# A chunk of the second expert product moved from behind a branch to the end of the arm before it

## The chip, the cores and the metric

The kernel runs on one core of a Trainium2 chip. The metric is the device time of one execution in microseconds, the median of several runs. The engines are TensorE (PE in the profile, with PEld for the loading of its weights), VectorE (DVE), ScalarE (ACT), GpSimd (POOL) and SyncE (SP), which issues DMAs. Each works through its own queue in order and waits for the others by semaphores.

## The reference

```python
attn = sigmoid(q @ k.T / sqrt(64) - log(448))     # 4 batches, 12 heads, 448 x 64
x    = (attn @ v) as rows                         # 1792 tokens x 768
do   = x @ w_skip > 0                             # tokens that go to an expert
e    = argmax(x[do] @ w_gate)                     # one of 8 experts
gate = softmax value of that expert
x[do] += gate * (relu(x[do] @ w1[e]) @ w2[e])     # w1: 768 x 1024, w2: 1024 x 768
h    = x @ w_in                                   # 768 x 2048
out  = elu(h) @ w_out                             # 2048 x 768
```

All in float32. The kernel keeps this accuracy by splitting each operand into a high and a low part (`hi`, `lo`) and making three products: high by high, high by low, low by high.

## The kernel before

There are three stages: attention and the routing of tokens, the experts, and the last two products over all tokens. The change lies in the expert stage.

**Blocks and arms.** Tokens are sorted by expert into blocks of 256 slots, two halves of 128. How many blocks there are and how full each is is known on the chip alone, so `level(i, k)` (L1081) is a nest of branches. Each block takes one of three arms by the count `k`: the *single* arm (one half used, L1104), the *middle* arm (a full half and one of up to 64 tokens, `few`, L1096) or the *whole* arm (two full halves, `many`, L1100). In the profiled execution blocks 0 to 7 are whole, whole, middle, whole, middle, single, single, single.

**Where engines meet at a branch.** The code behind a branch must hold for either way through it. So each of the middle and whole arms has an `else` in which `rest()` (L1075) gives TensorE, ScalarE and VectorE one tiny instruction (L1077, L1078, L1079), and the code behind may wait for that instruction in place of what the arm would have done.

**Weights.** An expert's weights are eight chunks of 128 x 1536: 0 to 3 are w1, 4 to 7 are w2. SyncE loads them into 13 buffers. `split_w` (L722) makes the high part on ScalarE (L728, tile `whi`) and the low part on VectorE (L730, `wlo`). There are four pairs of split buffers, so chunk c takes the pair of chunk c - 4. `ahead` (L806) splits two chunks ahead of the products.

**A block, in the order of TensorE's queue.** `between` (L956) turns the block's rows of x: `columns` makes three groups of four 128 x 128 turnings, into `pt0`, `pt1` and `acc1`; ScalarE and VectorE split each into `x2` (L762, L763). Behind that stand chunks 5 and 6 of the *previous* block's first half (`back`, L860), the splits of chunks 0 and 1, and, behind the next branch in `lead_in`, chunk 7. Then the arm: the product with w1 (chunks 0 to 3), relu to `h2`, the product with w2 (chunks 4 to 7). In the single and middle arms the first product leaves rows, so h is turned into columns by `h_columns` (L770), half by half of F: for chunks 4 and 5 after chunk 2, for chunks 6 and 7 late in the arm. ScalarE and VectorE then write its high and low parts (L785, L786). A half of 128 tokens takes four groups of three products per w2 chunk (L737, L738, L739); a half of 64 takes four of two (L801, L802).

The first half's w2 product (`h` = 0 in the code) is spread so that TensorE has work across the branch: chunk 4 at the arm's end, 5 to 7 behind the next turning. The second half's stands wholly in the arm. `outcome` (L908) adds the gated sum to the rows on VectorE (L916); in the middle arm TensorE first doubles it up (L915), from a copy that ScalarE makes (L866). In block 0 `slot_order` (L1036) makes the order of the remaining rows: 12 small products into `acc1`, and seven VectorE instructions behind them (L1043 to L1054).

What sets the order of all this is the order of the code: TensorE, ScalarE and VectorE are scheduled by hand here.

Of the kernel before, what the change touches and what calls it, by code (L numbers as in the profile page):

```python
# [23 lines left out]
P = 128  # L24
# [10 lines left out]
KF1 = F1 // P  # L35
# [6 lines left out]
N2 = DM // 2  # L42
WCH = 1536
FA = 9
TB = 4
NOR = NTT // TB * TB
# [43 lines left out]
def build(nc, tc, a):  # L90
# [3 lines left out]
    with ExitStack() as top:  # L94
# [42 lines left out]
        def flip(dst, src):  # L137
            nc.tensor.transpose(dst, src, ident)  # L138
# [33 lines left out]
        with ExitStack() as st:  # L172
# [423 lines left out]
            for k_, p in enumerate(counted):  # L596
                nc.tensor.matmul(
                    ordered, ones_b, p, start=(k_ == 0), stop=(k_ == len(counted) - 1)
# [59 lines left out]
        with ExitStack() as st:  # L658
# [7 lines left out]
            def tiles(pool, names, shape, dt=F32):  # L666
                return [pool.tile([P, *shape], dt, name=n) for n in names]
# [16 lines left out]
            acc_t = tiles(psb, [f"acc{j}" for j in range(6)], [512])  # L684
            ends = (*pt_t, acc_t[1])
            py = [[acc_t[j][:, :N2] for j in js] for js in ((2, 3), (4, 1))]
# [81 lines left out]
                    split_columns(g, ends[g], x2)  # L768

            def h_columns(nh, sizes):  # L770
                for h, n in enumerate(sizes):
                    pt = pt_t[(nh + h) % 2].rearrange("p (c n) -> p c n", c=4)[:, :, :n]
                    for j in range(4):
                        w = slice(j * P, (j + 1) * P)
                        if n == P:
                            flip(pt[:, j, :], hs_t[nh][:, w])
                        else:
                            nc.tensor.matmul(
                                pt[:, j, :], hf_t[nh][:, w], fold[:, :n], start=True, stop=True
                            )  # L780
                    f, t = slice(4 * nh, 4 * nh + 4), slice(h * P, h * P + n)
                    h_hi, h_lo = h2[:, 0, f, t], h2[:, 1, f, t]
                    if n < P:
                        h_lo = h2[:, 0, f, h * P + n : (h + 1) * P]
                    nc.scalar.activation(h_hi, pt, AF.Relu)  # L785
                    nc.vector.scalar_tensor_tensor(  # L786
                        h_lo, pt, 0.0, h_hi, op0=ALU.max, op1=ALU.subtract
                    )

            def product(o, h, n, a2, i, c, width, k0, total):  # L790

                t = slice(h * P, (h + 1) * P)
                for j in range(WCH // width):
                    w = slice(j * width, (j + 1) * width)
                    hi, lo = (u[:, w] for u in weights(i, c))
                    a_hi, a_lo = a2[:, 0, k0 + j, t], a2[:, 1, k0 + j, t]
                    first, last = k0 + j == 0, k0 + j == total - 1
                    if n == P:
                        gemm(o, a_hi, a_lo, hi, lo, first, last)
                    else:  # L800
                        nc.tensor.matmul(o, a_hi, hi, start=first, stop=False, skip_group_check=True)  # L801
                        nc.tensor.matmul(  # L802
                            o[:n], a_hi[:, :n], lo, start=False, stop=last, skip_group_check=True
                        )
# [52 lines left out]
                        else:  # L857
                            nc.scalar.copy(hf_t[nh], acc_t[(3, 0)[nh]])

            def back(i, h, n, chunks):  # L860

                for c in chunks:
                    c4, nh = divmod(c - 4, 2)
                    product(py[nh][h], h, n, h2, i, c, N2, 4 * c4, KF1)
                    if n < P and c4:
                        nc.scalar.copy(yf_t[nh], py[nh][h])  # L866

            def expert(i, sizes, following=None):
                whole = sizes == (P, P)
                aside = places_in_order() if i == 0 else iter(())  # L870

                def soon():
                    if i:
                        outcome(i - 1, 0, P)

                if i == 0:
                    split_w(0, 1)
                if whole:
                    up_two(i, aside, soon)
                    ahead(i, 4)  # L880
                else:
                    up_parts(i, sizes, aside, soon)
                    if len(sizes) > 1:
                        skips(f"many{i}")
                    elif i + 1 < NB:
                        skips(f"more{i + 1}", (following + 3) >> 2)
                ahead(i, 5)
                if i == 0:
                    run(aside)
                    order_rows()  # L890
                for h, n in list(enumerate(sizes))[1:]:
                    if whole:
                        back(i, h, n, range(4, 8))
                        outcome(i, h, n)
                        back(i, 0, P, range(4, 5))
                    else:
                        back(i, h, n, range(4, 6))
                        h_columns(1, sizes)
                        back(i, h, n, range(6, 8))
                        back(i, 0, P, range(4, 5))  # L900
                        outcome(i, h, n)
                if i == 0:
                    slot_order()
                if len(sizes) == 1:
                    back(i, 0, P, range(4, 5))
                    h_columns(1, sizes)

            def outcome(i, h, n):  # L908

# [46 lines left out]
            def between(i, more):  # L956

                if i == 0 and more:
                    return
                if i == 1 and not more:  # L960
                    gather(1)
                columns(i)
                if i == 0:
                    return
                back(i - 1, 0, P, range(5, 7))
                if more:
                    split_w(i, 0)
                    split_w(i, 1)
                else:
                    back(i - 1, 0, P, range(7, 8))  # L970
                    outcome(i - 1, 0, P)
                    scatter(i - 1)
# [62 lines left out]

            def slot_order():  # L1036

                og = acc_t[1][:, :NOR]
                for t in range(NOR):
                    nc.tensor.matmul(  # L1040
                        og, one_hot[:, t], ca[:, t], start=(t == 0), stop=(t == NOR - 1)
                    )
                nc.vector.tensor_copy(order_off, og)  # L1043
                for j in range(4):
                    nc.vector.scalar_tensor_tensor(
                        slot_off,
                        fill[:, 3 - j : NHB + 7 - j],
                        order_off[:, j : j + 1],
                        slot_off,
                        op0=ALU.mult,  # L1050
                        op1=ALU.add,
                    )
                nc.vector.tensor_scalar_add(slot_ext, slot_off, float(NT))
                nc.vector.tensor_scalar_add(order, order_off, float(NT))  # L1054
# [292 lines left out]
```

## Time and profile before

| | us |
|---|---|
| median of 3 runs | 949.8 (947.25 to 951.26) |
| the profiled execution | 948.0 |
| its span | 946.2 |
| attention and routing | 0 to 214.5 |
| experts | 214.5 to 464.2 |
| last two products | 464.2 to 946.2 |

A time in a timeline is counted from the start of the span. TensorE's products are pipelined: a row's duration reaches into the next product, so the pace is read from one start to the next. "Idle before" is the time in which the engine had nothing running, and the arrow names what ended it. "Issue" means that the profile shows nothing that it waited for.

### The profile page before, as it was taken

What the parts mean: (1) busy time and instruction counts of PE and PEld (TensorE: products, weight loads), DVE (VectorE), ACT (ScalarE), POOL (GpSimd) and SP (SyncE); (2) the same over time, 40 slices, a digit from 0 to 9 for tenths busy, and PEclk for the clock granted to TensorE, in tenths of its full rate; (3) what the DMA queues carried; (4) which work ended last, traced back from release to release, by engine and by line L of the source; (5) the groups of instructions that cost most, each with busy time, mean ns of one, the idle gap of its engine ahead of it and who ended that gap; (6) DMA issues with size and microseconds to landing.
All of it is one profiled execution on the core that took longest, in us unless ns stands there. A gap on an engine that the chain in (4) does not pass through costs nothing.

```text
span 946.2 us, 13964 instructions
## 1 busy us (share of the span) xinstructions
PE 910.7 (96%) x5331; PEld 754.2 (80%) x5331; DVE 585.6 (62%) x893; ACT 504.6 (53%) x703; POOL 72.3 (8%) x69
## 2 busy tenths in 40 slices
PE   7999999999999999999799999999999999999998
PEld 4555555549997898888799999888888888888997
DVE  3787877957656456688388888533443444434664
ACT  7777777535345346577254455434443434443664
POOL 0000000010220110234100000000000100000100
PEclk9999999999999999999999999999999999999999
DMA  9989887579962683594663333000010100000100
GB/s 247 266 254 269 248 272 228 168 242 417 357 258 70 251 295 111 207 410 174 222 201 100 104 101 113 34 34 1 17 34 17 55 13 1 1 1 1 68 1 34
DMA packets 33992, 139.50 MB, mean 147 GB/s; under 512 B 4874, under 2 KB 5514, under 8 KB 33890
## 3 DMA queue, kind: packets, MB, share of 16 engines
q1 hardware_dynamic: 29410, 119.17, 37.8%
q0 software_dynamic: 4480, 19.01, 5.8%
q8 instruction: 59, 0.97, 0.4%
q14 instruction: 43, 0.35, 0.1%
HBM read 117.58 MB, written 23.60 MB: 149 GB/s over the span
## 4 chain that ended last, share of the span: by engine, by line
PE 83%; DVE 3%; issue 2%; ACT 2%; DMA 1%; SPq 0%; ACTq 0%; DVEq 0%
PE acc L1220 15%; PE pt L1220 9%; PE acc L1187 8%; PE acc L1188 8%; PE acc L1189 8%; PE acc L737 6%; PE acc L738 6%; PE acc L739 6%; PE ps L239 3%; PE po L253 3%; PE pt L138 1%; PE acc L801 1%; PE acc L802 1%; PE acc L138 1%; DMA raw<-in_wi 1%
## 5 line engine op out<-in xcount | busy, mean ns | idle before, releaser
L730 DVE TENSOR_TENSOR wlo<-raw,whi 128x1536 fp32r<-128x1536 f32 x64 | 111.3, 1756 | 34.6 <-ACT whi L728 34.2
L1198 DVE SCALAR_TENSOR_TENSOR m<-m,acc 128x512 f32<-128x512 f32 (+1 forms) x64 | 39.7, 621 | 143.9 <-ACT m L1197 143.9
L1196 ACT ACTIVATE m<-acc 128x512 f32<-128x512 f32 (+1 forms) x64 | 34.9, 546 | 171.5 <-PE acc L1189 171.5
L1187 PE MATMUL acc<-x,wih 128*128 128x256 f32 (+1 forms) x360 | 121.1, 336 | 0.0
L1188 PE MATMUL acc<-x,wih 128*128 128x256 f32 (+1 forms) x360 | 121.1, 336 | 0.0
L1189 PE MATMUL acc<-x,wil 128*128 128x256 f32 (+1 forms) x360 | 120.7, 335 | 0.0
L728 ACT CAST whi<-raw 128x1536 fp32r<-128x1536 f32 x64 | 94.0, 1482 | 25.0 <-DMA raw<-in_w 9.1
L246 ACT ACTIVATE at<-ps,bias 112x896 f32<-112x896 f32 x96 | 89.1, 1009 | 29.1 <-PE ps L239 29.1
L1220 PE MATMUL acc<-wol,gh 128*128 128x256 f32 x320 | 101.0, 316 | 0.0
L1220 PE MATMUL acc<-woh,gl 128*128 128x256 f32 x320 | 100.5, 314 | 0.0
L1220 PE MATMUL acc<-woh,gh 128*128 128x256 f32 x320 | 100.4, 314 | 0.0
L253 PE MATMUL po<-at,vt 112*64 112x448 f32 x384 | 77.5, 545 | 0.7 <-DVE xT L261 0.7
L239 PE MATMUL ps<-qs,kh 128*112 128x448 f32 x192 | 73.3, 382 | 3.0 <-ACT kh L232 1.5
L1177 DVE TENSOR_TENSOR wol<-wo,woh 128x768 fp32r<-128x768 f32 x64 | 61.2, 956 | 23.4 <-ACT woh L1176 23.0
L239 PE MATMUL ps<-qs,kl 128*112 128x448 f32 x192 | 71.6, 373 | 2.6 <-DVE kl L233 2.6
L1189 PEld LDWEIGHTS acc<-x,wil 128*128 128x128 f32 x360 | 68.0, 189 | 7.4
L1187 PEld LDWEIGHTS acc<-x,wih 128*128 128x128 f32 x360 | 68.0, 189 | 6.3
L1188 PEld LDWEIGHTS acc<-x,wih 128*128 128x128 f32 x360 | 67.9, 189 | 5.9
L1220 PEld LDWEIGHTS acc<-woh,gh 128*128 128x128 f32 x320 | 60.3, 188 | 10.1
L1220 PEld LDWEIGHTS acc<-wol,gh 128*128 128x128 f32 x320 | 60.3, 188 | 9.3
L1176 ACT CAST woh<-wo 128x768 fp32r<-128x768 f32 x64 | 53.4, 834 | 26.0 <-PE acc L1220 25.9
L1202 DVE TENSOR_TENSOR gl<-m,gh 128x512 fp32r<-128x512 f32 (+1 forms) x64 | 40.0, 626 | 40.5 <-ACT gh L1201 40.5
(252 smaller groups left out, 2034.7 us busy)
## 6 DMA issues: line engine op xcount, KB each, us to landing
raw<-in_w SPq DMA_DIRECT2D x66, 768.0 KB, 10.6
kr<-in_k SPq DMA_DIRECT2D x22, 448.0 KB, 6.7
raw<-in_wi SPq DMA_DIRECT2D x9, 768.0 KB, 6.8
raw<-in_wo SPq DMA_DIRECT2D x9, 768.0 KB, 6.5
vt<-in_v SPq DMA_DIRECT2D x12, 448.0 KB, 6.3
x_d<-xr SPq DMA_DIRECT2D x14, 384.0 KB, 3.4
raw<-in_wi SPq DMA_DIRECT2D x14, 384.0 KB, 3.1
raw<-in_wo SPq DMA_DIRECT2D x14, 384.0 KB, 3.1
```

The costliest lines, as they stand in the source:

```text
L239: nc.tensor.matmul(ps[:CP, j, :S], kk[:, 2 * p + j, c * CP : (c + 1) * CP], qs[:, p, j], start=(i == 0), stop=(i == 1),)
L246: nc.scalar.activation(at[:, :, c, :], ps[:CP, :, :S], AF.Sigmoid, bias=bias[:CP], scale=QK_SCALE)
L253: nc.tensor.matmul(po[64 * j : 64 * j + 64, :S], vt[:, 2 * (hp % 2) + j, c, :], at[:, j, c, :], start=(c == 0), stop=(c == NCH - 1),)
L728: nc.scalar.copy(w_hi, raw)
L730: nc.vector.tensor_sub(w_lo, raw, w_hi)
L737: nc.tensor.matmul(o, a_hi, b_hi, start=first, stop=False)
L738: nc.tensor.matmul(o, a_hi, b_lo, start=False, stop=False)
L1177: nc.vector.tensor_sub(pair[1], wo_r[f], pair[0])
L1187: nc.tensor.matmul(o, a, b, start=(cc == 0), stop=False)
L1188: nc.tensor.matmul(o, a, c, start=False, stop=False)
L1189: nc.tensor.matmul(o, wil[:, cc], b, start=False, stop=(cc == KD - 1))
L1220: nc.tensor.matmul(o, a, b, start=(clears and f == 0 and k_ == 0), stop=(f == KF2 - 1 and k_ == 2), skip_group_check=True,)
```

## The change

1. Chunk 5 of the first half (12 products) leaves `between` and is placed at the end of each arm. In the whole arm it follows chunk 4. In the single arm it follows the late turning of h. In the middle arm one half of it stands before `outcome` and one half behind.
2. In the middle arm the late turning of h comes before chunk 5 of the second half, not behind it, and chunk 4 of the first half before it. `h_columns` takes the second half first.
3. In block 0 `slot_order` stands before chunk 4 of the first half, and uses `acc0`.

```diff
             def h_columns(nh, sizes):
-                for h, n in enumerate(sizes):
+                for h, n in reversed(list(enumerate(sizes))):
...
-            def product(o, h, n, a2, i, c, width, k0, total):
+            def product(o, h, n, a2, i, c, width, k0, total, part=slice(None)):
...
-                for j in range(WCH // width):
+                for j in range(WCH // width)[part]:
...
-            def back(i, h, n, chunks):
+            def back(i, h, n, chunks, part=slice(None)):
...
-                    product(py[nh][h], h, n, h2, i, c, N2, 4 * c4, KF1)
+                    product(py[nh][h], h, n, h2, i, c, N2, 4 * c4, KF1, part)
...
-                for h, n in list(enumerate(sizes))[1:]:
-                    if whole:
-                        back(i, h, n, range(4, 8))
-                        outcome(i, h, n)
-                        back(i, 0, P, range(4, 5))
-                    else:
-                        back(i, h, n, range(4, 6))
-                        h_columns(1, sizes)
-                        back(i, h, n, range(6, 8))
-                        back(i, 0, P, range(4, 5))
-                        outcome(i, h, n)
+                start, end = slice(0, 2), slice(2, 4)
+                if whole:
+                    back(i, 1, P, range(4, 8))
+                    outcome(i, 1, P)
+                    if i == 0:
+                        slot_order()
+                    back(i, 0, P, range(4, 6))
+                    return
+                if len(sizes) > 1:
+                    back(i, 1, sizes[1], range(4, 5))
+                back(i, 0, P, range(4, 5))
                 if i == 0:
                     slot_order()
-                if len(sizes) == 1:
-                    back(i, 0, P, range(4, 5))
-                    h_columns(1, sizes)
+                h_columns(1, sizes)
+                if len(sizes) > 1:
+                    back(i, 1, sizes[1], range(5, 8))
+                    back(i, 0, P, range(5, 6), start)
+                    outcome(i, 1, sizes[1])
+                    back(i, 0, P, range(5, 6), end)
+                else:
+                    back(i, 0, P, range(5, 6))
...
-                back(i - 1, 0, P, range(5, 7))
+                back(i - 1, 0, P, range(6, 7))
...
-                og = acc_t[1][:, :NOR]
+                og = acc_t[0][:, :NOR]
```

How this moves TensorE's instructions, at two places. The end of the single arm of block 1 in the code (each block has the same three arms), before: the last turning of h (`hs`) into `pt`, the branch, and the first turning group of the next block's rows (`xg`).

```order
L138 MATMUL pt_1959<-cst,hs_1882 128x128 [waits Activation_49]
L138 MATMUL pt_1959<-cst,hs_1882 128x128 x3
L1093 UNCONDITIONAL_BRANCH
L1086 COMPARE_AND_BRANCH
L1073 REGISTER_ALU
L1343 BRANCH_PREFETCH_HINT
L138 MATMUL pt_1958<-cst,xg_1898 128x128 [waits DMASW4_49,DVE_49]
```

The same end after (`acc_1964` is the sum that chunk 5 goes into; each `...` stands for more of the same kind):

```order
L138 MATMUL pt_1959<-cst,hs_1882 128x128 [waits Activation_49]
L138 MATMUL pt_1959<-cst,hs_1882 128x128 x3
L737 MATMUL acc_1964<-whi_1890,h_1869 128x384
L738 MATMUL acc_1964<-wlo_1891,h_1869 128x384
L739 MATMUL acc_1964<-whi_1890,h_1869 128x384
...
L1098 UNCONDITIONAL_BRANCH
L1091 COMPARE_AND_BRANCH
L1078 REGISTER_ALU
L1348 BRANCH_PREFETCH_HINT
L138 MATMUL pt_1958<-cst,xg_1898 128x128 [waits DMASW4_49,DVE_49]
```

The 12 products of chunk 5 now stand between the turning of h and the turning of x; behind the turning of x chunk 6 follows at once.

The end of the middle arm after, from the last products of chunk 7 of the second half (`acc_1961`); `hf` is ScalarE's copy, L920 the doubling, L1082 the tiny product of the branch, and the last row the first product of a whole arm:

```order
L802 MATMUL acc_1961<-wlo_1887,h_1869 64x384
L737 MATMUL acc_1964<-whi_1890,h_1869 128x384
...
L920 MATMUL acc_1960<-hf_1883,cst 128x384 [waits Activation_49]
L920 MATMUL acc_1961<-hf_1884,cst 128x384 [waits Activation_49]
L737 MATMUL acc_1964<-whi_1890,h_1869 128x384
...
L1101 UNCONDITIONAL_BRANCH
L1082 LDWEIGHTS iota_h
L1082 MATMUL acc_1965<-iota_h 128x2
L1101 UNCONDITIONAL_BRANCH
L1105 COMPARE_AND_BRANCH
L737 MATMUL acc_1960<-x_1868,whi_1892 128x256 [waits DVE_49,PE_49,Activation_49]
```

Before, chunk 4 of the first half stood where the first six of these products stand, and nothing stood between the doubling and the branch. The last row's wait for VectorE is in the code of both.

## Rows read from the trace of the kernel before

**Rows 1.** Stages: us, busy (x instructions) of PE PEld DVE ACT POOL, clock, DMA, GB/s.
```profile
214.50:464.17 249.67, 234.71 (x1457) 217.66 (x1457) 164.78 (x192) 132.59 (x153) 46.01 (x34) 0.99 0.66 252
464.17:946.20 482.03, 477.44 (x2844) 423.50 (x2844) 262.72 (x425) 226.38 (x377) 18.38 (x19) 1.00 0.16 50
```

**Rows 2.** TensorE's waits from 205 to 470: us in total, times, longest.
```profile
PE pt L138 <- DVE h L786: 4.4, 3, 1.5
PE acc L1187 <- issue: 3.9, 1, 3.9
PE pt L138 <- issue: 2.1, 1, 2.1
PE acc L737 <- DVE rest L1079: 1.9, 1, 1.9
PE acc L801 <- DVE h L786: 1.9, 2, 0.9
PE pt L138 <- DVE order L1054: 1.3, 1, 1.3
PE pt L138 <- DVE rest L1079: 1.0, 1, 1.0
```

**Rows 3.** Chunks 5 to 7 ahead of blocks 3, 1, 6: columns as in rows 1.
```profile
317.30:325.15 7.85, 7.85 (x39) 7.69 (x38) 5.36 (x6) 3.87 (x5) 2.54 (x2) 0.81 1.00 399
245.22:251.59 6.37, 6.37 (x40) 6.21 (x39) 4.78 (x5) 3.90 (x5) 5.15 (x5) 1.00 0.99 388
410.36:416.73 6.37, 6.37 (x39) 6.37 (x38) 4.91 (x5) 5.27 (x5) 1.55 (x1) 1.00 1.02 415
```

**Rows 4.** Timeline, TensorE, end of block 6: start, us, instruction, idle before and releaser.
```profile
428.11 0.60 PE L138 MATMUL pt<-cst,xg 128*128 128x128 f32 x4
430.17 0.66 PE L138 MATMUL pt<-cst,xg 128*128 128x128 f32 x4 [1.46 <-DVE h L786]
...
431.02 0.42 PE L737 MATMUL acc<-whi,h 128*128 128x384 f32 x1
```

**Rows 5.** Single block 5 as a stretch: columns as in rows 1.
```profile
396.06:416.73 20.67, 19.21 (x105) 17.25 (x105) 17.96 (x16) 15.37 (x15) 7.14 (x5) 1.00 1.02 412
```

**Rows 6.** Timeline, VectorE, from block 6's first split to its h.
```profile
412.69 3.43 DVE L730 TENSOR_TENSOR wlo<-raw,whi 128x1536 fp32r<-128x1536 f32 x2 [0.58 <-ACT whi L728]
416.54 1.76 DVE L730 TENSOR_TENSOR wlo<-raw,whi 128x1536 fp32r<-128x1536 f32 x1 [0.42 <-ACT whi L728]
...
419.27 3.41 DVE L730 TENSOR_TENSOR wlo<-raw,whi 128x1536 fp32r<-128x1536 f32 x2
423.12 1.76 DVE L730 TENSOR_TENSOR wlo<-raw,whi 128x1536 fp32r<-128x1536 f32 x1 [0.44 <-ACT whi L728]
424.79 0.68 DVE L786 SCALAR_TENSOR_TENSOR h<-pt,h 128x512 fp32r<-128x512 f32 x1
```

**Rows 7.** Timeline, TensorE, third product of chunk 4 in block 6.
```profile
425.91 0.34 PE L739 MATMUL acc<-whi,h 128*128 128x384 f32 x1
```

**Rows 8.** Timeline, TensorE, middle block 2 behind the late turning of h.
```profile
307.31 0.45 PE L801 MATMUL acc<-whi,h 128*128 128x384 f32 x1 [0.93 <-DVE h L786]
```

**Rows 9.** Timeline, TensorE, the turning behind middle block 4.
```profile
388.32 1.09 PE L138 MATMUL pt<-cst,xg 128*128 128x128 f32 x8 [1.01 <-DVE rest L1079]
```

**Rows 10.** Timeline, TensorE, the turning behind whole block 0.
```profile
242.46 0.64 PE L138 MATMUL pt<-cst,xg 128*128 128x128 f32 x4
244.37 0.66 PE L138 MATMUL pt<-cst,xg 128*128 128x128 f32 x4 [1.28 <-DVE order L1054]
```

**Rows 11.** Timeline, VectorE, ahead of whole block 1.
```profile
247.59 3.42 DVE L730 TENSOR_TENSOR wlo<-raw,whi 128x1536 fp32r<-128x1536 f32 x2 [0.57 <-ACT whi L728]
250.93 0.14 DVE L1079 COPY rest<-cst 128x1 f32<-128x1 f32 x1
```

**Rows 12.** Timeline, TensorE, the turning behind middle block 2.
```profile
315.86 1.06 PE L138 MATMUL pt<-cst,xg 128*128 128x128 f32 x8 [2.10 <-issue]
```

**Rows 13.** Line 1100, TensorE's sequencer (PEldq): duration ns min/median/max, first and last start.
```profile
L1100 PEldq COMPARE_BRANCH  x10: 63/192/3501, 210.2 to 385.2; - x10
```

## The prediction

> **What bounds the kernel now.** I read the page first, then the table by stage, then TensorE's waits inside the expert stage, then single instructions around each wait. By stage [rows 1] the expert stage lasts 249.7 us with TensorE busy for 234.7, and the last stage is busy for 477.4 of its 482.0. So TensorE sets the end, and what the expert stage loses moves the end one for one. The reader should look for what is left to win: 15.0 us of idle time in a stage whose products are the same before and after. Its waits are few and have names [rows 2]: three for the second half of h in the single arm (4.4 us), two for the same thing in the middle arm (1.9), one for the row order after block 0 (1.3), one for VectorE's last copy of a block (1.0), one with no releaser that the profile shows (2.1), and two that lie outside the change: 1.9 at the start of block 0 and 3.9 at the jump out of the stage. None is a wait for a DMA, so I cost the weight loads at nothing. The waits which the change can reach make 8.6 us, 10.7 with the one that has no releaser.
>
> **What the change does to each wait.** The executed blocks are whole, whole, middle, whole, middle, single, single, single (0 to 7). Chunk 5 is 12 products. Thirty-six products take 6.37 us at the full clock [rows 3], so 12 take 2.12 and 24 take 4.25. These 2.12 us are only moved: from behind the next block's turning of x to the end of the arm. The question at each place is what they cover now, and what they no longer cover where they stood.
>
> *Single arm, three times.* The first turning group of the next block starts at 428.11, the second at 430.17, 2.06 later [rows 4]. The second and third together take 0.85 (430.17 to 431.02), 0.43 each. So the wait for VectorE's h costs 2.06 - 0.43 = 1.63. With 12 products in between it is gone: h is wanted 2.12 us later than now.
>
> What is late next is VectorE. It is busy for 17.96 of the block's 20.67 us [rows 5], and without the 1.63 the block would last 19.04. I walk its queue for block 6. B is the first product behind the turning (410.36), T the first product of the new block (416.73) [rows 3]. VectorE starts splitting the new block's first two chunks at 412.69, B + 2.33, and has done chunks 0 to 4 and the gated sums at 419.27 + 3.41 = 422.68; taking off the 0.42 that it waited for chunk 2, that is 9.57 us of work in a row [rows 6]. Chunk 5 adds 1.67 (423.12 to 424.79) and h's first half 0.68. So h can be ready at B + 2.33 + 9.57 + 1.67 + 0.68 = B + 14.25. Today T is B + 6.37, h is done 8.74 after T (425.47), and the third product of chunk 4, which reads it, starts 9.18 after T (425.91) [rows 7]: it is in time by 0.44. With chunk 5 gone from between B and T, T is B + 4.25 and h is ready at T + 10.0, while the product still stands at T + 9.18. A new wait of 0.8 us. So a single block gains 1.63 - 0.82 = 0.81, and the three 2.4 us. The bounds of one are 0 and 1.63.
>
> *Middle arm, twice.* Now the two halves of chunks 4 and 5 go first, then h is turned, and the next product waits 0.93 [rows 8]. After the change, chunk 5's half stands between the turning and the first product that reads h: 8 products of 0.18, 1.4 us, longer than the wait. The smaller half is also turned first. I take both waits as gone, 1.9 us. The turning itself stands behind chunk 4 of both halves; what it reads was copied long before. The new place of the gated sums needs ScalarE's copy of the half before, covered by half of chunk 5 (1.06 us). Uncovered, it could cost about what the wait in [rows 8] costs, 0.9; I take nothing.
>
> *The second middle arm's end.* The next turning starts at 388.32 after a wait of 1.01 for VectorE's last copy, which stands behind the gated sums [rows 9]. The sums now come 1.06 us before the arm's end: I take 1.0 as won.
>
> *Block 0's end.* The turning's second group starts 1.91 behind the first [rows 10], 1.48 more than 0.43, for the row order. The order's products now stand ahead of 24 others (4.25 us): the 1.48 is gone. But block 1 is whole, and the first product of a whole arm waits for VectorE's last copy ahead of it (the 1.9 at block 0's start is that wait [rows 2]). The copy stands behind the splits of chunks 0 and 1 and ends at 250.93 + 0.14 = 251.07 [rows 11], B + 5.85 with B at 245.22 [rows 3]. Today T is B + 6.37 and nobody sees it. With 24 products T would be B + 4.25, and the copy holds it to about B + 5.95. Of the 2.12 moved out only 0.42 comes back, 1.70 is a new wait. Block 1: 1.48 - 1.70 = -0.2.
>
> *Block 3, whole too.* Its B to T took 7.85, at a mean clock of 0.81 [rows 3], because TensorE stood still for 2.10 before the turning [rows 12]. The same copy holds T to B + 5.95: 1.90 comes back of 2.12, another -0.2. The 2.10 itself I leave in place. Among the jumps of the branch that ends the arms, TensorE's sequencer has a median of 0.19 us and one of 3.50 [rows 13]. I read that one as this gap: a jump whose code was not there.
>
> *Into middle blocks 2 and 4* nothing changes: 2.12 move from one side of the turning to the other, and chunk 0's low part (B + 2.33 + 1.76 = B + 4.09) is in time for T = B + 4.25, and it is the second product that reads it. This is tight, by 0.2 and one product.
>
> *Sum.* 2.4 + 1.9 + 1.0 - 0.2 - 0.2 = 4.9 us. The profiled execution took 948.0 (span 946.2 and 1.8 around it), so 943.1 by its own time; against the median of 949.8 it is 944.9. The runs before lie between 947.25 and 951.26.
>
> **The rivals.** *Nothing takes the place of the waits.* If VectorE is not late, each wait goes in full: 3 x 1.63 + 1.9 + 1.0 + 1.48 = 9.3, 940.5. For it: VectorE stands still in the single arm between h and the next x, so there is some play. Against it: the 0.44 us of slack are all that rows 6 and 7 show where it counts, and 2.12 are taken out.
>
> *The jump behind the first middle arm finds its code.* The change makes the code longer, so each jump's target lies elsewhere. Then the 2.10 go too and the clock does not fall; since the copy holds block 3 to B + 5.95 either way, I add 2.1 to the sum: 7.0, 942.8. For it: half of the ten jumps took 0.19 or less [rows 13], and no other end of an arm shows such a wait [rows 2]. Against it: nothing in the trace says why this one missed.
>
> *More jumps miss (slower than before).* The same mechanism the other way. A miss costs 2.10 where the next block is whole and held by the copy anyway, and 2.10 plus 7.85 - 6.37 = 1.48 for the lower clock, 3.6 together, ahead of a middle or single block. There are four more such ends, of blocks 0, 1, 3 and 4. One more miss leaves 4.9 - 2.1 = 2.8 or 4.9 - 3.6 = 1.3 (947.0 or 948.5). From two on the gain is lost: 4.9 - 5.7 = -0.8, 950.6; with all four, 4.9 - 12.9 = -8.0, 957.8. Against it: today only one of these five ends shows the wait [rows 2]. For it: the single arm, which the jump passes over, becomes 12 products longer, and a whole level 24. [...]
>
> **Chances.** The forecast 0.45 (943.4 to 946.5, with a fall of the clock behind the new wait of 1.70 in block 1 at the upper end); waits gone in full 0.15; the long jump gone 0.15; one more miss 0.15; two or more 0.10. About 0.5% (4.75 us, up to 945.05) is what a measurement of this kernel can tell from no change, and my forecast lies almost on that line. Faster: half of the forecast and the two rivals below it, 0.50. Same: the other half, one miss and most of two, 0.45. Slower: 0.05. The range goes from waits gone in full, 940.5, to 949.5, which takes in one more miss.
>
> **What would show it.** Right: no wait for the order, for h ahead of the turning, or in the middle arm; in their place, in whole blocks 1 and 3 a wait of some 1.7 us ahead of the first product, for VectorE's last copy (in block 3 shorter if the clock is low there), and in the three single blocks 0.8 us at the third product of chunk 4, for h. Single blocks every 19.9 us, not 20.7 and not 19.0. Wrong: these two new waits missing; a jump of over 2 us at another block's end; or turning in the middle arm that still waits.

## The result and the profile after

The changed kernel takes 955.86 us (median of 6 runs, 953.83 to 956.70), the kernel before 947.82 beside it (6 runs, 946.58 to 951.26): a ratio of 1.0081, 95% interval 1.0066 to 1.0097. It is slower, and the time lies outside the range forecast. The profiled execution has a span of 953.9 against 946.2, so 7.7 us have to be found.

By stage, columns as in [rows 1]; the second row answers to the first of [rows 1], the third to the second:

```profile
0.00:216.16 216.16, 197.49 (x1031) 112.21 (x1032) 158.04 (x276) 145.55 (x173) 8.27 (x17) 0.99 0.80 242
216.16:470.24 254.08, 237.41 (x1456) 219.90 (x1456) 163.97 (x192) 130.65 (x153) 43.81 (x34) 0.97 0.65 247
470.24:953.90 483.66, 477.90 (x2844) 423.77 (x2844) 262.73 (x425) 226.33 (x377) 18.61 (x19) 0.99 0.16 50
```

The expert stage got 4.4 us longer (254.08 to 249.67). It begins 1.7 later (216.16 to 214.50), which is not the change: over the runs below its first product starts anywhere from 212.1 to 217.0. The last stage is 1.6 longer.

TensorE's waits in and around the expert stage, as in [rows 2]:

```profile
PE acc L1192 <- issue: 4.4, 1, 4.4
PE acc L737 <- issue: 3.9, 1, 3.9
PE acc L737 <- DVE rest L1084: 3.5, 2, 1.9
PE acc L1082 <- issue: 2.9, 1, 2.9
PE pt L138 <- issue: 2.5, 2, 2.0
PE acc L739 <- DVE h L786: 1.2, 2, 0.6
PE acc L1194 <- issue: 1.1, 1, 1.1
```

Of the waits that the change aimed at, none is left: no h ahead of a turning, no h in the middle arm, no order, no copy behind block 4. In their place are the two that were forecast. The timeline has one at the start of whole block 1, and one at chunk 4's third product in blocks 6 and 7:

```profile
252.83 0.36 PE L737 MATMUL acc<-x,whi 128*128 128x256 f32 x1 [1.55 <-DVE rest L1084]
433.80 0.44 PE L739 MATMUL acc<-whi,h 128*128 128x384 f32 x1 [0.55 <-DVE h L786]
453.67 0.45 PE L739 MATMUL acc<-whi,h 128*128 128x384 f32 x1 [0.61 <-DVE h L786]
```

Waits with a named releaser fell from 4.4 + 1.9 + 1.3 + 1.0 = 8.6 us to 1.55 + 0.55 + 0.61 = 2.7, leaving out the one ahead of block 0. That wins 5.9. What takes it back has no releaser ("issue"). Timeline of TensorE: ahead of block 3's first product, at block 5's turning, and between block 5's chunks 6 and 7.

```profile
324.67 0.19 PE L1082 MATMUL acc<-iota_h 128*128 128x2 f16 x1 [2.87 <-issue]
392.44 1.06 PE L138 MATMUL pt<-cst,xg 128*128 128x128 f32 x8 [1.98 <-issue]
399.97 0.69 PE L737 MATMUL acc<-whi,h 128*128 128x384 f32 x1 [3.90 <-issue]
```

With 0.51 at block 7's end and the 4.44 of the jump out of the stage, these gaps come to 13.7 us. Before they were 2.10, 0.42 and 3.89, together 6.4: 7.3 more. And behind two of them, where TensorE had stood still, the granted clock is low: 0.59 and 0.74 of full speed on the mean over the stretches below, and in the trace's clock record 0.50 from 323.94 to 330.76 and from 399.03 to 405.86, with 1.00 on either side. Stretches with the same products in pairs (block 1's first 36 against block 3's; block 6's chunk 7 with its first 27 against block 5's), columns as in [rows 1]:

```profile
252.83:257.31 4.48, 4.48 (x38) 4.48 (x39) 2.96 (x4) 2.86 (x2) 0.00 (x0) 1.00 1.01 410
325.00:332.07 7.07, 7.07 (x38) 7.07 (x39) 4.48 (x4) 2.79 (x2) 1.30 (x2) 0.59 1.01 404
...
421.78:430.20 8.42, 8.42 (x40) 7.12 (x40) 8.21 (x7) 7.69 (x7) 1.78 (x1) 1.00 0.96 354
...
399.97:411.13 11.16, 11.16 (x40) 9.70 (x41) 5.91 (x5) 4.86 (x4) 4.19 (x4) 0.74 1.02 409
```

7.07 - 4.48 = 2.6 and 11.16 - 8.42 = 2.7 are lost to the clock, 5.3 against the 1.5 of [rows 3]. So the stage is -5.9 + 7.3 + 3.8 = +5.2 by these three, and +4.4 by the stages; 0.8 I leave unassigned. The last stage's 1.6 has a gap of the same kind in it (1.1, the last row of the waits).

That the sequencer stood at jumps is told by the sources of the three branches (duration ns min/median/max, first and last start): L1098 is the jump into the single arm, L1101 the one over the middle arm, L1105 the one over the whole arm and the jump that follows it. Before, their longest took 1952, 431 and 3501 ns (the last is [rows 13]).

```profile
L1098 PEldq COMPARE_BRANCH  x8: 68/70/5879, 207.6 to 439.3; - x8
L1101 PEldq COMPARE_BRANCH  x7: 66/211/6073, 212.9 to 387.7; - x7
L1105 PEldq COMPARE_BRANCH  x10: 63/250/3471, 213.3 to 388.4; - x10
```

The 6073 is the gap of 2.87, the 3471 that of 1.98, the 5879 that of 3.90. A gap is shorter than its jump: the jump of 6.07 begins at 318.54, and TensorE's products ran on until 321.80. What the jumps wait for is in the page's third part, one line for each kind of queue (packets, MB, share):

```profile
q8 instruction: 61, 1.00, 0.4%
```

These are fetches of code: 1.00 MB in 61 of them is 16 KB each. That they are TensorE's, and that the jumps wait for them, is told by the times in the traces' records (start and end, us):

```
                          jump               last fetch ahead of its end   from the fetch's end to the jump's
before, behind block 2    311.81 to 315.31   312.93 to 313.81              1.50
changed, ahead of block 3 318.54 to 324.61   322.23 to 323.18              1.43
changed, behind block 4   388.40 to 391.87   389.50 to 390.38              1.49
changed, in block 5       394.03 to 399.91   397.54 to 398.56              1.35
```

The same holds for each of the 57 jumps of TensorE over 2 us in the 14 traces of this text: it ends 1.35 to 1.63 us behind the end of such a fetch. The jump of 5.88 has a second fetch in it, at 395.31. I call what one fetch brings a code page. How many instructions that is can be counted in the last stage, where TensorE takes no jump: in the changed kernel 241 to 267 of its instructions start from one fetch to the next, 5362 in the 21 pages from 492.52 to 944.57, 255.3 on the mean; in the kernel before 255.1 in 20. I take a page for 256, and the runs below test that.

### The profile page after: what moved, and what is told of

The parts are those of the page before. It is cut to its first block, busy times and chain, and to the rows that moved or that the text cites. A ratio compares the mean times of both kernels' runs of the same rounds, so it can differ in the third digit from the quotient of the medians.

```text
span 953.9 us, 13959 instructions
## 1 busy us (share of the span) xinstructions
PE 912.8 (96%) x5331; PEld 755.9 (79%) x5331; DVE 584.7 (61%) x893; ACT 502.5 (53%) x703; POOL 70.7 (7%) x69
## 4 chain that ended last, share of the span: by engine, by line
PE 82%; issue 3%; DMA 2%; DVE 2%; ACT 1%; SPq 0%; ACTq 0%; DVEq 0%
PE acc L1225 15%; PE pt L1225 9%; PE acc L1192 8%; PE acc L1194 8%; PE acc L1193 8%; PE acc L737 6%; PE acc L739 6%; PE acc L738 6%; PE ps L239 4%; PE po L253 3%; PE pt L138 1%; PE acc L801 1%; PE acc L802 1%; PE acc L138 1%; DMA raw<-in_wi 1%
## 5 line engine op out<-in xcount | busy, mean ns | idle before, releaser
L737 PE MATMUL acc<-whi,h 128*128 128x384 f32 x176 | 61.8, 351 | 3.9 <-issue 3.9
```

Source lines behind the costliest of these rows:

```text
L737: nc.tensor.matmul(o, a_hi, b_hi, start=first, stop=False)
```

## Experiments: does the place of the code matter?

The theory was that the gaps are code fetches at jumps, and that they depend on where the borders of code pages fall. The rival was that they belong to the work: weight loads, buffers, or the moved products. In the first test the kernel before gets instructions that are never executed, so that the code behind them lies further on and nothing executed changes:

```diff
+            def filler(i, arm):
+                for _ in range(FILL.get((i, arm), 0)):
+                    nc.tensor.matmul(acc_t[5][:, :2], iota_h, iota_h[:, :2], start=True, stop=True)
...
                         expert(i, (P,), following)
+                        filler(i, "single")
```

Each product is two instructions (the profile's page counts 5331 products and 5331 weight loads). 38 products at the end of block 0's single arm:

> The kernel before, with 38 small TensorE products (76 instructions) added at the end of block 0's single arm, which is never executed: all code behind it lies 76 instructions further on, nothing executed differs. Theory (the gaps without a releaser are fetches of code, and what they cost depends on where the borders of TensorE's 256-instruction code pages fall between a jump and its target): the two jumps in a row at the end of block 2 now have their targets in one page, so the 2.1 us ahead of block 3's turning go, and with them the 1.5 of low clock behind it: 947.8 - 3.6 = 944.2. One doubt on record: a page border now lies between the start of block 3 and its jump over the middle arm, where the changed kernel waits 2.9; if it waits here too, 947 to 950. Rival (the gaps belong to the work around them, such as weight loads or buffers, not to the place of the code): no change, 947.8 within 1, with 2.1 in the same place.

Measured: 959.67, ratio 1.0131 (1.0100 to 1.0162). Its waits without a releaser, and the branches over the middle (L1102) and the whole arm (L1107):

```profile
PE acc L1196 <- issue: 4.3, 1, 4.3
PE acc L740 <- issue: 2.7, 1, 2.7
PE acc L1078 <- issue: 2.4, 1, 2.4
PE acc L1198 <- issue: 2.2, 1, 2.2
```

```profile
L1102 PEldq COMPARE_BRANCH  x7: 66/216/5639, 209.9 to 387.7; - x7
L1107 PEldq COMPARE_BRANCH  x10: 63/198/397, 210.3 to 388.4; - x10
```

The pair of jumps behind block 2 is cured as forecast (longest 0.40 where it was 3.50), and the doubt on record came true: block 3's jump now takes 5.64. Two more gaps, in block 5 (2.7) and in the last stage (2.2), nobody had foreseen. The one in block 5 is not at its jump, which took 0.92 here, but behind it, at the last product of chunk 7: a fetch lies at 399.52 to 400.42, and the product starts 1.51 behind its end. So a fetch cost 2.7 here without a slow jump. That the place of the code matters was right, and the sign was wrong: 76 instructions that never run cost 12 us. With 200:

> The kernel before, with 100 small TensorE products (200 instructions) at the same never executed place. Theory (fetches of code): the second of the two jumps in a row crosses a page border at the end of block 2 and now at the end of block 4 as well: 2.1 us stay ahead of block 3's turning, and some 2 come ahead of block 5's (in place of the 1.0 that it waits there for VectorE), with a stretch at half the clock, 1.5: 947.8 + 2.5 = 950.3. Rival (the gaps belong to the work around them): 947.8 within 1 and no gap without a releaser behind block 4.

Measured: 958.02, ratio 1.0090 (1.0058 to 1.0123).

```profile
L1102 PEldq COMPARE_BRANCH  x7: 66/221/5865, 211.9 to 390.4; - x7
L1107 PEldq COMPARE_BRANCH  x10: 63/324/3181, 212.3 to 391.2; - x10
```

In the records both pairs of jumps are slow, as forecast (3.12 behind block 2, 3.18 behind block 4), and block 1's jump (5.87) and block 5's (6.62), which were not forecast, join them: hence 958.0 and not 950.3. The control is a filler of exactly 256, in both kernels, in block 0's middle arm:

> The kernel before with 128 small TensorE products (256 instructions, one page) in block 0's middle arm, which is never executed. All code behind it lies exactly one page further on, so every later jump and target has its old place within a page. Theory (what counts is the place within a 256-instruction page): unlike with 76 or 200 instructions the waits are those of the kernel before, 2.1 us with no releaser ahead of block 3's turning and none over 1 us elsewhere before the jump out of the stage; 948.3 and up to 2 more, since the jump over the filled arm now passes a page more. Rival (any added code costs, by its length or by chance): 951 to 960, with gaps in other places.

> The changed kernel with the same 256 instructions at the same place. Theory: its own gaps again, in their places (2.9 ahead of block 3, 2.0 and 3.9 ahead of and inside block 5's start), 955.9 and up to 2 more. Rival: gaps in other places, a time that differs by more than 3.

Measured: 947.54, ratio 0.9997 (0.9974 to 1.0021), and 956.11, ratio 1.0074 (1.0050 to 1.0097): each the time of its own kernel without the filler. The waits of the second:

```profile
PE acc L738 <- issue: 5.1, 1, 5.1
PE acc L1201 <- issue: 4.3, 1, 4.3
PE acc L1083 <- issue: 3.9, 2, 2.7
PE pt L139 <- issue: 2.3, 3, 1.4
```

They stand at the changed kernel's places: 5.1 in block 5, 2.7 ahead of block 3, 1.4 at block 5's turning. (The other 1.2 at L1083 is at block 0, where the jump over the filled arm now takes 2.49.) In the first of the two the pair behind block 2 is slow again (2.98), though the profile puts the wait behind it down to VectorE's last copy (1.6): the turning starts 0.56 behind the jump's end, where it was 0.55 in the kernel before. So 76 and 200 instructions cost 12 and 10 us and 256 cost nothing. The rival that added code costs by its length falls.

## Experiments: borders alone, or also the time between hint and jump?

`skips` puts a hint for a jump into TensorE's code some way ahead of it (BRANCH_PREFETCH_HINT; in the changed kernel 18 are executed, of 28 to 47 ns). In the changed kernel chunk 5 no longer stands between the hint for the jump into the single arm and that jump. First only the place was changed, by 10 instructions; in the second kernel h is made ahead of chunk 5's split as well:

> The changed kernel with 5 small TensorE products (10 instructions) at the end of block 0's single arm, never executed. Theory (fetches of code): 10 instructions are enough to put the border between the two jumps at the end of block 2 (a gap of some 2.1 ahead of block 3's turning comes) and to take it from between those at the end of block 4 (the 2.0 ahead of block 5's turning goes); block 3's jump over the middle arm then lies in the same page as the block's start (its 2.9 and the low clock behind it, 2.6, go), and block 5's jump into the single arm has its fetch sooner (3.9 and 2.6 of low clock go, or a part of it). 955.9 - 13.9 + 3.6 = 945.6, between 943 and 950. Rival (the change itself makes these gaps, because 12 products fewer stand between the hint for a jump and the jump, wherever the pages lie): 3.9 and 2.9 stay, 952 to 956.

Measured: 954.42, ratio 1.0055 (1.0021 to 1.0089). The forecast of 945.6 was far off. Timeline, TensorE:

```profile
317.15 0.88 PE L139 MATMUL pt<-cst,xg 128*128 128x128 f32 x6 [0.49 <-issue]
326.19 0.18 PE L1083 MATMUL acc<-iota_h 128*128 128x2 f16 x1 [3.48 <-issue]
399.07 0.44 PE L738 MATMUL acc<-whi,h 128*128 128x384 f32 x1 [3.56 <-issue]
```

The gap at block 5's turning went, as forecast, but the 2.1 forecast ahead of block 3's turning did not come (0.49, the first row), and the gaps ahead of block 3 and in block 5 stayed, as the rival said. So either borders alone do not explain them, or the borders did not lie where I had counted them: this run can't tell which.

> The kernel of the run before this one, and in the single arm VectorE and ScalarE turn the first half of h ahead of splitting chunk 5, not behind it; TensorE's order is the same. Theory (the 0.55 to 0.61 us at the third product of chunk 4 are VectorE's queue: h stands behind 1.7 us of splitting): these waits go, three times 0.6, single blocks every 19.3 us and not 19.9: 1.8 faster than the run before it. Rival (VectorE is the bound of the single arm, so the wait only moves to the next thing that VectorE makes): the single blocks stay at 19.9, no difference.

```diff
+                        sooner = nh == 1 and c3 == 0 and len(sizes) == 1
+                        if sooner:
+                            h_columns(0, sizes)
                         ahead(i, c + 1)
-                        if nh == 1 and c3 == 0:
+                        if nh == 1 and c3 == 0 and not sooner:
                             h_columns(0, sizes)
```

Measured: 953.63, ratio 1.0069 (1.0043 to 1.0094), no different from the run before it. The wait moved from chunk 4's third product to the next turning, once in each single block:

```profile
438.09 0.66 PE L139 MATMUL pt<-cst,xg 128*128 128x128 f32 x4 [0.57 <-DVE h L787]
...
457.87 0.66 PE L139 MATMUL pt<-cst,xg 128*128 128x128 f32 x4 [0.60 <-DVE h L787]
```

The blocks are 457.87 - 438.09 = 19.78 apart, against 19.81 (423.90 to 443.71) in the changed kernel. The rival's forecast holds: this change of order only moved the wait to the next thing that VectorE makes, and the blocks take as long as before.

Now the time alone, with every instruction but the hint in its place, in the kernel before:

```diff
-                    skips(f"two{i}", k >> 1)
...
-                back(i - 1, 0, P, range(5, 7))
+                back(i - 1, 0, P, range(5, 6))
+                if more:
+                    skips(f"two{i}", k >> 1)
+                back(i - 1, 0, P, range(6, 7))
```

> The kernel before, with one instruction moved: the hint for the jump into the single arm stands behind chunk 5's product (12 products, 2.1 us) and not ahead of the turning of x. The code is as long as before, and no jump, target or product has another place. Theory (a hinted jump is free only when its hint stands some 5.8 us ahead of it; with chunk 5 gone the changed kernel's hints stand 1.8 to 4.0 us ahead): the hints stand some 2.7 us ahead of the jumps into blocks 5, 6 and 7, and each of these jumps takes 3 to 6 us of TensorE's sequencer where two of the three took 0.4: a gap of 2 to 4 us with low clock behind it at one to three of them, 947.8 + 4 to + 12: about 954. Rival (only the page borders count, and they are where they were): 947.8 within 1, jumps of 0.4.

Measured: 950.75, ratio 1.0037 (1.0023 to 1.0052): slower, by less than forecast. Timeline, TensorE, in blocks 5 and 6:

```profile
394.36 0.44 PE L737 MATMUL acc<-whi,h 128*128 128x384 f32 x1 [1.21 <-issue]
416.84 0.44 PE L737 MATMUL acc<-whi,h 128*128 128x384 f32 x1 [1.55 <-issue]
```

And the reverse in the changed kernel: chunk 7 ahead of the jump instead of behind it.

```diff
-                back(i - 1, 0, P, range(6, 7))
+                back(i - 1, 0, P, range(6, 8) if more else range(6, 7))
```

> The changed kernel with the first of those edits alone: the jump into the single arm stands behind chunk 7's product. Nothing is done about page borders: the two jumps that end a middle arm have a border between them behind block 4, and block 3's start has one ahead of its jump over the middle arm. Theory (both matter, distance and borders): the jumps into blocks 6 and 7 take 0.4 and not 2.0, and block 5's 3.9 falls to under 1; behind block 4 2 us stay, ahead of block 3 2.5 to 3 with 2.6 of low clock stay: 955.9 - 5.5 = 950.4, between 948 and 953. Rival (borders alone): the jump into block 5 still costs 3 or more, 954 to 957.

Measured: 950.96, ratio 1.0033 (1.0008 to 1.0058), within the forecast, but in part by luck: block 5's gap was to fall to under 1 and is 2.52 (put down to a split of ScalarE, but the product starts 0.17 behind the jump's end), and the gap ahead of block 3 is 4.81, not 2.5 to 3. From the traces' records, us from the hint to the jump into the single arm, and what the jump took:

```
                                  block 5        block 6        block 7
before                            6.42  0.44     5.95  0.44     5.97  1.95
changed                           1.80  5.88     3.74  2.03     3.75  0.44
before, hint behind chunk 5       3.00  3.10     2.20  4.18     2.03  1.48
changed, jump behind chunk 7      3.88  5.91     5.52  0.69     5.46  0.43
```

One instruction moved by 12 products makes two jumps of 0.44 into 3.10 and 4.18, and leaves the third about as it was; 12 products put back make 2.03 into 0.69. The first is the cleaner test, since nothing else moves: the kernel before with 256 more instructions, which leave the borders in place, repeats its row with 0.43, 0.44 and 2.75. In the second the borders move too, because chunk 7 stood in both arms of the branch and now stands once ahead of it. Block 5's jump stays at 5.91 there: the pair of jumps ahead of it missed (longest 3.43), and the hint was again only 3.88 ahead. Two causes, then: what stands between a hint and its jump, and where the borders fall.

The records also show why the distance counts. The fetch for block 6's jump begins 3.68 us behind the hint in the kernel before (405.97 to 409.65), 3.30 in the changed one (415.69 to 418.99) and 3.89 with the hint late (410.40 to 414.29). In the changed kernel 3.30, then 1.10 for the fetch and 1.37 from its end to the jump's make 5.77; the hint stands 3.74 ahead, and the jump takes the 2.03 that are missing.

## Experiments: is there a version that beats both?

Beside the later jump, the middle arm's last products go between the two jumps that end it, and fillers are set against the borders:

```diff
                         with arm.Else():
                             rest()
+                            last_of_middle(i)
```

> The changed kernel with three edits that leave its order of products and copies as it is. First, the jump into the single arm stands behind chunk 7's product and not ahead of it, so that its hint is again some 6 us ahead. Second, the last products of the middle arm (chunk 5 of its first half, and the gated sums) stand between the two jumps that end it. Third, 60 instructions that are never executed behind block 0, 30 in block 6 and 40 ahead of the last stage, set so that no page border lies between the start of a block and its jump over the middle arm, and none soon behind the start of the last stage. Theory (all that the changed kernel lost is fetches of code, and its moved products gain the 4.9 us that were forecast): no wait of more than 1 us without a releaser before the jump out of the stage; the gain of 4.9 and the 3.6 that the kernel before lost behind block 2: 947.8 - 4.9 - 3.6 = 939.3, between 937 and 943. Rival (the moved products themselves cost, by waits or the clock): over 947.

Measured: 948.35, ratio 0.9994 (0.9978 to 1.0010), a miss. Block 3's jump (1.51) and the pair behind block 2 were cured, but behind block 4 two jumps now took 3.16 and 3.07 (a border 27 instructions ahead of one of them is my count of the code, which no trace shows), and block 5's jump took 6.44:

```profile
397.77 0.47 PE L738 MATMUL acc<-whi,x 128*128 128x512 f32 x1 [3.76 <-issue]
```

A second fit of the fillers, alone and with one move more:

```diff
-                if i == 0:
-                    split_w(0, 1)
+                split_w(i, 1)
...
                     split_w(i, 0)
-                    split_w(i, 1)
```

> The same numbers of never executed instructions, the splits of chunk 1 where the changed kernel has them. Theory (block 5 lost 3.8 us and 1.7 of low clock to the jumps behind block 4, where a border stood 27 instructions ahead of one jump and between the two others): these go, the two waits of 1.6 for VectorE's last copy stay: 948.3 - 5.5 = 942.8. Rival (the fit of the borders can't be foreseen): within 2 of the run before, 946 to 950.

> The kernel of the run before (three cures), with other numbers of never executed instructions (60 behind block 0, 120 in block 3, 70 in block 5, 72 in block 6, 60 ahead of the last stage), set so that the two jumps behind block 4 have their targets in one page and a page border comes right behind the hint of each jump into a single arm; and with the splits of chunk 1 on ScalarE and VectorE behind the jumps of the arms and not ahead of them, so that VectorE's last copy of a block stands behind one split and not two. Theory (the first products of whole blocks 1 and 3 wait 1.6 each because that copy stands behind chunk 1's split, as the prediction said, and the rest of the loss is fetches): both waits go, 3.2; the 3.8 at block 5 and its low clock go: 948.3 - 3.2 - 5.5 = 939.6, between 937 and 943. Rival (the copy is late whatever stands ahead of it, or chunk 1's split is now late itself): as the next run, about 943.

Measured: 944.19, ratio 0.9948 (0.9928 to 0.9967), and with the split moved 941.63, ratio 0.9927 (0.9899 to 0.9955). The waits without the move, then with it, then the expert stage with it:

```profile
PE acc L1203 <- issue: 3.0, 1, 3.0
PE acc L740 <- DVE rest L1085: 2.7, 2, 1.6
PE acc L738 <- issue: 2.3, 2, 1.9
```

```profile
PE acc L1201 <- issue: 3.3, 1, 3.3
PE acc L738 <- ACT whi L729: 2.1, 2, 1.4
PE acc L738 <- DVE rest L1083: 1.9, 1, 1.9
PE pt L739 <- issue: 0.8, 1, 0.8
PE acc L740 <- DVE h L787: 0.6, 1, 0.6
```

```profile
214.81:456.13 241.32, 234.41 (x1456) 217.29 (x1457) 163.52 (x192) 130.76 (x153) 39.40 (x33) 0.99 0.67 256
```

The stage takes 241.32, against 249.67 before and 254.08 in the changed kernel. The 2.7 for VectorE's last copy is gone with the move, and the times differ by 2.6. So the step that put this wait down to chunk 1's split held. The 2.1 that the profile puts down to ScalarE's split, ahead of blocks 5 and 6, are not a price of the move: the splits of chunk 0 were done at 389.11 and 409.08, before TensorE stopped (391.21 and 411.11), and its products start 0.17 behind the end of two jumps of 3.46 and 4.08. Without the move the same two jumps (4.68 and 3.12) stand behind the 2.3 of "issue". Both kernels are faster than the kernel before, by 0.5 and 0.7%.

Do the cures do it alone? The kernel before, in its own order, with cures that suit it:

> The kernel before, in its own order of products, with the cures that suit it: its middle arm's last products (chunk 4 of the first half and the gated sums) between the two jumps that end the arm, the splits of chunk 1 behind the jumps, and never executed instructions (40 behind block 0, 90 in block 3, 126 in block 5, 100 in block 6, 100 ahead of the last stage) set against the page borders. Theory (the moved products are worth their 4.9 once code fetches are dealt with alike): this kernel wins only the 3.6 lost behind block 2, 948.3 - 3.6 = 944.7, and stays some 3 behind the kernel with the moved products and all cures (941.6), which still has up to 2 us of fetches. Rival (the cures bring all of it and the moved products nothing): 941.6 within 1.

Measured: 948.88, ratio 1.0007 (0.9991 to 1.0024): nothing won. So these cures do not bring all of it in this order, but my 944.7 was wrong too. The gap behind block 2 is gone; others came:

```profile
PE acc L738 <- ACT whi L729: 2.4, 1, 2.4
PE acc L738 <- issue: 1.9, 1, 1.9
```

The second is block 5's jump again (4.68). The first, in whole block 3, is put down to the moved split, but it is a fetch too: the weight load of that product, which carries the wait for ScalarE, started at 322.08, a fetch ran from 322.25 to 323.20, and the product came 1.52 behind its end, at 324.72. So this run is no clean measure of what the moved products are worth at equal fetches, and this order had one fit of the fillers where the changed kernel had two. The trace of the changed kernel (5.9 us of waits) is the best there is.

## Why the prediction was wrong

- **Forecast, and held.** Single blocks every 19.9 us (19.92 and 19.81, the first by luck: block 5 had no wait for h and ran at a mean clock of 0.95); a new wait for h at chunk 4's third product, 0.82 forecast, 0.55 and 0.61 measured; in whole block 1 a wait for VectorE's last copy, 1.70 forecast, 1.55 measured; no wait in the middle arm, none for the order, none for the copy behind block 4. The sum of these terms was 4.9; the waits fell by 5.9, more because blocks 3 and 5, held up by their jumps, showed no new wait of their own.
- **The step that failed.** "These 2.12 us are only moved ... The question at each place is what they cover now, and what they no longer cover where they stood." I asked that of the engines' waits and of nothing else, and put new jumps that miss at nothing in the sum. Where chunk 5 stood it lay between the hint for the jump into the single arm and that jump, and it covered code fetches that no row of before shows as a wait because they were hidden. Without it the hint for block 5's jump came 1.80 us ahead and not 6.42, and a jump of 0.44 became one of 5.88; block 6's came 3.74 ahead and not 5.95, and 0.44 became 2.03. In all the runs showed 7.3 us more of gaps without a releaser and 3.8 more of low clock, where the sum had no change. The trace of before held a sign of it that I passed over: its jump into block 7 took 1.95 with the hint 5.97 ahead, and TensorE waited 0.42 behind it.
- **How the loss divides is open.** The late hint alone cost the kernel before 2.5 us (950.75 against 948.25). The slow jump ahead of block 3 (5.64) and the slow pair behind block 4 (3.18) also came with chunk 5 in its old place, when 76 and 200 instructions that never run had moved the borders. So these two gaps may be no more than where the changed code lies, and no run says how much of the 8.0 us is which.
- **The rival that came.** "More jumps miss" was the right mechanism, with the wrong chance (0.25 in all) and only half of its condition. I took it for a draw of borders alone; for the jumps into the single arms the time that the change takes away made it likely. It counted the ends of four blocks, and one of the three large gaps stands at such an end (1.98, behind block 4); the other two stand at jumps behind the turning, which it did not count. Its price was too low as well: 2.10 and 1.48 of clock each, against 2.87 + 2.6, 1.98, and 3.90 + 2.7.
- **The 2.10 "I leave in place"** did not stay: it went from block 2's end (the pair there now took 0.20) and two others came.
- **What a hint brought.** In the kernel before the jumps into blocks 5 and 6 took 0.44 with hints 6.42 and 5.95 ahead, and fetches began between hint and jump (at 385.91 and 389.06, and at 409.65). These jumps pass over a middle and a whole arm, which in blocks 2 and 3 are 278 and 403 instructions in the records, together 2.7 times the 255 of one fetch. So I read the last fetch ahead of each as that of the jump's target, an estimate: no record shows which code a fetch brought.

What stays open: in the best kernel the hints stand 5.0 to 5.5 us ahead, and the jumps into blocks 5 and 6 still took 3.46 and 4.08 in the records, with 0.72 and 1.38 of idle time behind them: their fetches began 6.14 and 6.81 us behind the hint, not 3.3 to 3.9, and no run shows why. Distance helps, then, but it does not suffice. Whether the weight loads on the DMA engines delay these fetches was not tried.

## What to carry to other kernels

Where a program has branches, a product between a hint and its jump can be cover, like a product ahead of a wait (here 12 fewer between the two turned jumps of 0.44 into 3.10 and 4.18): before moving it, note how far ahead of each jump the hint stands. Before a change of a per cent or two is put down to its order of work, shift the code by a filler that never runs, and by one of exactly a page (here 256 instructions: ratios 1.0131 and 1.0090 with 76 and 200, 0.9997 with 256); if the first moves the time and the second doesn't, the difference may be only where the code lies. "Issue" gaps at one line, with a branch of microseconds beside them, were the sign here (gaps of 1.98 to 3.90 at branches of 3.47 to 6.07); so was a wait put down to an engine that had long been done (ScalarE's splits in the best kernel, done 2.1 and 2.0 us before TensorE stopped).

## What the runs showed that I had not expected

The size of it: instructions that are never executed moved this kernel by 0.9 to 1.3%, more than the whole change was meant to win, and 256 of them by nothing (0.9997). One missed jump took TensorE's sequencer 2.9 to 3.5 us where the fetch began 0.6 to 1.1 us behind the jump's start, and 5.6 to 6.7 in the worst cases between blocks, where the last fetch began 3.2 to 4.4 us behind it. In block 5 of the changed kernel two fetches followed each other (395.31 and 397.54), but the jump of 6.07 ahead of block 3 holds only one, at 322.23; why it began so late was not tried. And a gap of 2.9 to 3.9 cost nearly as much again in the clock behind it (2.6 and 2.7).
